# Two-layer attention kernel: for some query tiles the maxima of the first two key chunks are taken as a + relu(b − a) in one pass of VectorE

## The chip, the core and the metric

One NeuronCore of a Trainium2 chip runs the whole program. The time is device microseconds (us) from start to end of one execution; a figure for a kernel is the median of several. The profile is of one execution and has its own time. Engines: PE is TensorE, which multiplies matrices into PSUM banks of 128 x 512 fp32; DVE is VectorE, ACT is ScalarE, POOL is GpSimd, SP only issues DMAs.

## The reference

Four blocks in a row on x of 2048 tokens by 512: A, B, A, B with the same weights. B (a router that sends two tokens through a small feed-forward net) matters here only because two rows of x, and with them two keys, are known late.

```python
# A: attention of 32 heads of 16, one shared key and value head (x is already normalised)
q = (x @ wq).reshape(B, S, H, Dh).transpose(0, 2, 1, 3)
k = x @ wk
v = x @ wv
scores = einsum("bhqd,bkd->bhqk", q, k) * (Dh ** -0.5)
p = softmax(scores, axis=-1)
o = einsum("bhqk,bkd->bhqd", p, v)
return o.transpose(0, 2, 1, 3).reshape(B, S, H * Dh) @ wo
```

## The kernel before

`layer` runs one A and one B block; it is called twice. A layer has 32 units `u` (4 query chunks x 4 groups of heads x 2) of 16 steps each, so 512 steps `t` of about 2.5 us.

The softmax subtracts each row's exact maximum, so every score is computed twice:

- **Maxima.** `max_mm(mi, n)` multiplies 128 queries by one chunk of 512 keys (`CW`) into a bank of the pool `psM` (4 banks), and VectorE reads the bank and reduces it to one column of the tile `mx` (L404, L406). There are four key chunks; a tile `mi` holds two of them for two halves of the rows: even `mi` have chunks 0 and 1, odd `mi` chunks 2 and 3. `n` from 0 to 3 gives the half and the chunk: the half is `h = 1 - n % 2`, the chunk `2 * (mi % 2) + n // 2`. Half 0 lies on the array's rows 0 to 47, half 1 on rows 64 to 111.
- **`max_parts`** (L414) takes the largest of the four chunks on VectorE and splits it in two parts on GpSimd (L419, L420); **`max_rows`** turns it on TensorE (L426), copies it on ScalarE (L428) and sends it by SP's DMA into two more rows of `q_st` (L432), so that the next product subtracts the maximum by itself.
- **Scores.** `scores(t, i)` computes keys by queries into a bank of `psS` (3 banks, L453), and ScalarE takes the exponential into `pr` (L455). Quarter `i` of a step lies on half `i % 2` of the rows.
- **`pv_mm`** multiplies by the values into `pO` (L482). **`between`** puts pieces of other projections (queries of the next unit, output projection; L187) on TensorE.

The order is written by hand. A step has four quarters `i`; each issues one `scores` and then one max product of the tile that is `LEAD` = 12 steps ahead (`made(mi) = mi - 12` from tile 16 on). After every third quarter (`RUN` = 3, counted over the whole layer as `4 * t + i`) come `pv_mm` for three halves of `pr` and perhaps one piece. So TensorE's work goes in *runs*: three pairs (score product, max product), then `pv_mm`, then perhaps a piece. The two products of a pair lie on different halves of the rows.

Before step 0 of a layer, eight steps issue max products alone; `first` gives the order of the first ones. Between the layers `layer` waits for B's two tokens and then corrects two columns of the keys (L1177 to L1188) and of the values (L1196, L1197).

Keys: `kv_piece` computes a chunk into `kvs[c]`, `k_store` writes it to DRAM, `k_spread` reads it back in six DMAs of SP into the rows of `k_sts`.

Of the kernel before, what the change touches and what calls it, by code (L numbers as in the profile page):

```python
# [9 lines left out]
F32 = mybir.dt.float32  # L10
BF = mybir.dt.bfloat16
FR = mybir.dt.float32r
U32 = mybir.dt.uint32
AF = mybir.ActivationFunctionType
OP = mybir.AluOpType
# [30 lines left out]
HALVES = 3  # L46

# [7 lines left out]
def interleaved_layers(ctx, tc, x_in, wq, wkv, wo, w_r, w_gate, w_up, w_down, out):  # L55
# [57 lines left out]
    k_sts = [work.tile([P, S], FR, name="k_st", bufs=2) for _ in range(2)]  # L113

    x2_d = dram.tile([S, D], F32, name="x2_d")
    z_d = [dram.tile([2 * TPC, CW], F32, name=f"z_d{i}") for i in range(2)]
    zr_d = [dram.tile([2 * TPC, CW], F32, name=f"zr_d{i}") for i in range(2)]
    k_d = [dram.tile([P, 2, P], F32, name=f"k_d{i}") for i in range(NCH)]
# [169 lines left out]
    def k_spread(li, c):  # L288

        for i in range(2 * NSLOT):  # L290
            n, h = divmod(i, 2)
            r = h * HR + n * DH
            src = k_d[c].rearrange("(j x) m t -> x m j t", j=TPC)[:DH, n // 2]
            dst = k_sts[li][r:r + DH, c * CW:(c + 1) * CW].bitcast(F32).rearrange("x (j t) -> x j t", j=TPC)
            nc.sync.dma_start(dst, src)

    def kv_v(li, c):
        kf = kvs.pop(c)[0]
        pv = aux([P, TPC, 2 * DH], F32)
        nc.tensor.transpose(pv.rearrange("p j x -> p (j x)"), kf, ident)  # L300
        nc.scalar.copy(v_exts[li][:, c * TPC:(c + 1) * TPC, 1:32:2], pv[:, :, DH:])
# [60 lines left out]
    def layer(li, src_d, dst_d, early=None):  # L362
# [26 lines left out]
        mx, mi = {}, 0  # L389

        def max_mm(mi, n):
            u, i = divmod(mi, 16)
            if i == 0 and n == 0:
                mx[u] = work.tile([P, 4, 16], F32, name="mx", bufs=3)
            pm = bank()
            nq = cuts[u]

            b, r = divmod(i, 16 // nq)
            x, c = divmod(r, 2)
            j, s = divmod(x, 4 // nq)  # L400
            h, c = 1 - n % 2, 2 * c + n // 2
            q = (b * 4 // nq + s) * P
            r = slice(h * HR, h * HR + KQ)
            nc.tensor.matmul(pm, q_st[u][r, j, q:q + P], k_st[r, c * CW:(c + 1) * CW], start=True, stop=True)  # L404
            i = b * 16 // nq + h * 8 // nq + 2 * s + j
            nc.vector.reduce_max(mx[u][:, c, i:i + 1], pm, axis=AX.X)  # L406
# [388 lines left out]
        for c in range(NCH):  # L795
# [31 lines left out]
            for b in range(TPC):  # L827
# [9 lines left out]
                if li == 0:  # L837
                    t += 4 if c < NCH - 2 else 3
                    at(t, next_x, i, nc.gpsimd)
                    at(t + 2, ln_t, i)  # L840
                    if b == TPC - 1:
                        at(t + 4, whole, kv_piece, c)
                        at(t + 6, k_store, li + 1, c)
                        at(t + 6, kv_v, li + 1, c)
                        at(t + 8, k_spread, li + 1, c)
        wd, wu = [], []

        def load_wd(n):
# [5 lines left out]
            else:  # L854
                for k in range(2):
                    if n == 3:
                        w = work.tile([P, D], F32, name="so0", bufs=8)
                    elif n < 6:
                        w = work.tile([P, D], F32, name=("qh", "ql")[n - 4])
                    else:  # L860
                        w = work.tile([P, D], F32, name="wd", bufs=4)
# [64 lines left out]
        first[12:12] = [(4, n) for n in range(4)]  # L926
# [3 lines left out]
        for t in range(-LEAD0, last):  # L930
# [4 lines left out]
            mms = [(m, n) for m in tiles for n in range(4)]  # L935
            mms = [first[4 * m + n] if 4 * m + n < len(first) else (m, n) for m, n in mms]
# [230 lines left out]
        for tok in toks:  # L1167
            of = nc.snap(tok // P)
            xb.append((of, work.tile([P, NDC, P], F32, name="xh", bufs=3)))
            nc.gpsimd.tensor_copy(xb[-1][1], xT[:, :, bass.ds(of * P, P)])  # L1170
        q_st.clear()
# [20 lines left out]
        q_stack(0, 0, w, engs=both)  # L1192
        for of, x in xb:
# [42 lines left out]
    in_stats(g4, g4)  # L1236
    kv_v(0, 1)
# [7 lines left out]
    def early():  # L1245
# [3 lines left out]
        kv_v(0, 3)  # L1249
        k_spread(0, 3)  # L1250

# [32 lines left out]
```

## Time and profile before

| | |
|---|---|
| time, median of 3 runs | 2792.49 us (2791.6 to 2792.81) |
| the profiled execution: its own time, and its span | 2793.8 us, 2792.0 us |
| busy share of PE, PE's weight loads, DVE, ACT, POOL | 99%, 57%, 93%, 82%, 26% |
| mean granted TensorE clock | 0.985 |
| max products and their reductions | 4096 of each |

The span runs from the first to the last instruction; 1.8 us of the execution lie outside it. The ends of matrix products are modelled, so PE's 99% doesn't say that it runs at its peak. The stream of steps takes about 60 to 1340 us in the first layer and 1450 to 2730 us in the second; between them and at the end stand the B blocks.

### The profile page before, as it was taken

The numbers are of one execution on the slowest core, as the hardware profiler recorded it, in microseconds if no ns is written. First come the engines' busy times: TensorE is split into PE (matmuls) and PEld (weight loads), VectorE is DVE, ScalarE is ACT, GpSimd is POOL, SyncE is SP. The second block draws the span as 40 slices with busy tenths as digits, with TensorE's granted clock in tenths as the row PEclk, the third lists the DMA queues.
The fourth block names the chain that finished last, engine by engine and source line by source line (L and its number), as shares of the span: only waits on it lengthen the run. The fifth ranks groups of instructions, "written<-read, shape, count | busy, mean of one in ns | idle before, by whom it ended". The sixth has DMA issues, their size and how long they took to land. (4 is left out here: it accounts for less than half of the span.)

```text
span 2792.0 us, 94326 instructions
## 1 busy us (share of the span) xinstructions
PE 2755.8 (99%) x39761; PEld 1602.5 (57%) x39761; DVE 2607.0 (93%) x4496; ACT 2294.5 (82%) x4705; POOL 720.3 (26%) x1756
## 2 busy tenths in 40 slices
PE   7999999999999999999999999999999999999999
PEld 4655555555555555555656555555555555555555
DVE  7999999999999999999669999999999999999994
ACT  2888888888888888888718888888888888888884
POOL 2100002022451116525510000021124421154262
PEclk8999999999999999999969999999999999999999
DMA  3011110000110001111400000100001100110113
GB/s 110 8 31 34 40 56 18 19 13 19 43 44 18 16 18 48 37 35 42 132 25 9 20 20 20 30 19 16 18 14 51 35 15 20 31 41 22 35 54 122
DMA packets 71386, 97.68 MB, mean 35 GB/s; under 512 B 22732, under 2 KB 32396, under 8 KB 70964
## 3 DMA queue, kind: packets, MB, share of 16 engines
q1 hardware_dynamic: 68098, 89.84, 11.2%
q8 instruction: 313, 5.13, 0.8%
q10 hardware_dynamic: 2354, 1.61, 0.2%
q14 instruction: 109, 0.89, 0.1%
q0 software_dynamic: 512, 0.20, 0.0%
HBM read 43.68 MB, written 17.77 MB: 22 GB/s over the span
## 5 line engine op out<-in xcount | busy, mean ns | idle before, releaser
L406 DVE TENSOR_REDUCE mx<-pM 128x1 f32<-128x512 f32 x4096 | 2508.5, 682 | 84.9 <-PE pM L404 67.5
L455 ACT ACTIVATE pr<-pS 128x512 f32<-128x512 f32 x4044 | 2133.6, 603 | 322.1 <-PE pM L404 232.9
L404 PE MATMUL pM<-k_st,q_st 48*128 48x512 f32 x4096 | 1390.5, 443 | 5.4 <-DVE mx L406 2.4
L453 PE MATMUL pS<-q_st,k_st 50*128 50x512 f32 (+1 forms) x4248 | 1357.2, 422 | 4.6 <-DMA q_st<-mr 2.2
L482 PE MATMUL pO<-pr,v_ext 128*32 128x128 f32 (+1 forms) x22528 | 1175.4, 328 | 2.2 <-ACT so L488 1.9
L453 PEld LDWEIGHTS pS<-q_st,k_st 50*128 50x128 f32 x4248 | 683.1, 186 | 468.4 <-ACT pr L455 265.9
L482 PEld LDWEIGHTS pO<-pr,v_ext 128*32 128x32 f32 x22528 | 562.6, 109 | 527.0 <-issue 347.8
L404 PEld LDWEIGHTS pM<-k_st,q_st 48*128 48x128 f32 x4096 | 669.0, 187 | 33.6 <-DVE mx L406 27.5
L419 POOL CAST mp<-ma 128x8 fp32r<-128x8 f32 (+1 forms) x136 | 26.0, 191 | 834.7 <-PE pM L404 460.9
L613 POOL TENSOR_TENSOR x<-x,qf 128x128 f32<-128x128 f32 x128 | 58.6, 459 | 545.0 <-ACT qf L612 545.0
L187 PE MATMUL pO<-xT,wq_sb 128*32 128x128 f32 x3584 | 180.0, 273 | 0.0
L345 POOL CAST qh<-qf 128x128 fp32r<-128x128 f32 x120 | 34.8, 290 | 513.4 <-ACT qf L344 483.3
L187 PE MATMUL pO<-wo_sb,so 128*32 128x128 f32 x2816 | 137.1, 273 | 0.0
L187 PEld LDWEIGHTS pO<-xT,wq_sb 128*32 128x32 f32 x3584 | 111.3, 110 | 34.0
L634 POOL TENSOR_TENSOR xh<-xh 128x128 f32<-128x128 f32 (+7 forms) x384 | 98.1, 255 | 30.1
L187 PEld LDWEIGHTS pO<-wo_sb,so 128*32 128x32 f32 x2816 | 86.7, 110 | 24.1
L696 POOL TENSOR_TENSOR xh<-xh 128x256 f32<-128x256 f32 (+8 forms) x216 | 66.6, 308 | 15.0
L428 ACT COPY mr<-pM 16x128 f32<-16x128 f32 (+1 forms) x136 | 34.6, 255 | 31.0 <-DVE mx L406 18.0
L346 POOL TENSOR_TENSOR ql<-qf,qh 128x128 fp32r<-128x128 f32 x120 | 55.0, 459 | 9.7
L488 ACT COPY so<-pO 128x256 f32<-128x256 f32 (+1 forms) x136 | 52.6, 387 | 2.1 <-PE pO L482 2.1
L680 POOL TENSOR_SCALAR xh<-x,mv,rs 128x512 f32<-128x512 f32 x24 | 49.9, 2077 | 0.0
L187 PE MATMUL pS<-wo_sb,so 128*32 128x128 f32 (+1 forms) x896 | 44.2, 330 | 0.0
(251 smaller groups left out, 940.5 us busy)
## 6 DMA issues: line engine op xcount, KB each, us to landing
q_st<-qh SPq DMA_DIRECT2D x244, 64.0 KB
q_st<-mr SPq DMA_DIRECT2D x512, 2.0 KB
q_st<-ql SPq DMA_DIRECT2D x122, 64.0 KB
zt<-zr_d SPq DMA_DIRECT2D x120, 64.0 KB
xl_d<-xh SPq DMA_DIRECT2D x28, 256.0 KB
pr<-in_w_up SPq DMA_DIRECT2D x12, 448.0 KB
x<-in_x SPq DMA_DIRECT2D x20, 256.0 KB
x_d<-x SPq DMA_DIRECT2D x16, 256.0 KB
```

Of the source, the lines that this page charges most:

```text
L187: nc.tensor.matmul(out[r], lhsT[:, r], rhs, start=start, stop=stop, skip_group_check=shared)
L346: nc.gpsimd.tensor_tensor(ql, qf, qh.bitcast(F32), op=OP.subtract)
L404: nc.tensor.matmul(pm, q_st[u][r, j, q:q + P], k_st[r, c * CW:(c + 1) * CW], start=True, stop=True)
L406: nc.vector.reduce_max(mx[u][:, c, i:i + 1], pm, axis=AX.X)
L453: nc.tensor.matmul(ps[:, k * 2 * w:(k + 1) * 2 * w], k_st[rows, kt * P:(kt + 1) * P], q_st[u][rows, :, b * w:(b + 1) * w], start=True, sto ...
L455: nc.scalar.activation(pr[hs][:, h, :], ps, AF.Exp)
L482: nc.tensor.matmul(po[u][32 * j:32 * (j + 1), b * w + q.start:b * w + q.stop], v_ext[:, kt, 1 - u % 2:33 - u % 2], p[:, j % 2, k, j // 2, ...
L488: nc.scalar.copy(so[u][:, b * w:(b + 1) * w], po[u][:, b * w:(b + 1) * w])
L613: nc.gpsimd.tensor_tensor(x1[i][:, w], x1[i][:, w], y, op=OP.add)
L634: g.tensor_tensor(t[:, :n], t[:, :n], t[:, n:2 * n], op=OP.add)
L680: eng.tensor_scalar(xl, x1[i], mv2[m][:, b, 0:1], rs2[m][:, b:b + 1], op0=OP.subtract, op1=OP.mult)
L696: nc.gpsimd.tensor_tensor(rp_t[i][:, :n], rp_t[i][:, :n], rp_t[i][:, n:2 * n], op=OP.add)
```

## The change

In some tiles the maximum of chunks 0 and 1 of a half is no longer found by two reductions. A fifth key chunk `k_dif` holds key chunk 1 minus key chunk 0. The product with it gives b − a; ScalarE writes relu(b − a) to the tile `over` in SBUF; the ordinary product with chunk 0 gives a; one `tensor_tensor_reduce` on VectorE adds `over` to it and reduces the sum by max: a + relu(b − a) is max(a, b). GpSimd sets the unused column of `mx` to -3e38. `pairs(mi)` says for how many halves of a tile this is done: one (half 1) for every sixth tile from 20 to 494, in both layers, and both halves for the eight even tiles below 16 in the second layer. In such tiles the order of `n` becomes 2, 0, 1, 3 or 2, 0, 3, 1. `first` of the second layer is rearranged so that tiles 0 and 2 come last. `k_dif` is made on GpSimd, stored and spread by SP like a chunk of keys, and its two late columns are corrected between the layers by products of their own (`xd`, `pd`, `kdn`). Three weight tiles of `load_wd` move to other buffers.

```diff
 RUN = 3
 HALVES = 3
 
+PAIR = 6
+PAIRED = 0, 16
...
     k_sts = [work.tile([P, S], FR, name="k_st", bufs=2) for _ in range(2)]
+    k_difs = [work.tile([P, CW], FR, name="k_dif", bufs=2) for _ in range(2)]
...
-    def k_spread(li, c):
+    def spread(of, dst):
 
         for i in range(2 * NSLOT):
             n, h = divmod(i, 2)
-            src = k_d[c].rearrange("(j x) m t -> x m j t", j=TPC)[:DH, n // 2]
-            nc.sync.dma_start(dst, src)
+            src = of.rearrange("(j x) m t -> x m j t", j=TPC)[:DH, n // 2]
+            nc.sync.dma_start(dst[r:r + DH].bitcast(F32).rearrange("x (j t) -> x j t", j=TPC), src)
+    def k_spread(li, c):
+        spread(k_d[c], k_sts[li][:, c * CW:(c + 1) * CW])
+
+    dif = []
+
+    def k_dif():
+
+        d = work.tile([P, P], F32, name="qf")
+        nc.gpsimd.tensor_tensor(d, kvs[1][0], dif.pop(), op=OP.subtract)
+        dif.append(d)
+
+    def k_dif_parts():
+        kf = dif.pop()
+        dif.append(work.tile([P, 2, P], FR, name="kp", bufs=1))
+        nc.gpsimd.tensor_copy(dif[0][:, 0, :], kf)
+        nc.gpsimd.tensor_tensor(dif[0][:, 1, :], kf, dif[0][:, 0, :].bitcast(F32), op=OP.subtract)
+
+    def k_dif_store():
+        nc.sync.dma_start(kd_d, dif.pop().bitcast(F32))
+
+    def k_dif_spread(li):
+        spread(kd_d, k_difs[li])
 
     def kv_v(li, c):
         kf = kvs.pop(c)[0]
+        if c == 0:
+            dif.append(kf)
         pv = aux([P, TPC, 2 * DH], F32)
...
+        mx, mi, over = {}, 0, {}
+
+        def pairs(mi):
+
+            c = mi % 2
+            if c:
+                return 0
+            if mi < PAIRED[li]:
+                return 2
+            return int(mi >= 16 and mi % PAIR == 2 and mi < 16 * (NU - 1))
+
+        def column(u, i, n):
+
             nq = cuts[u]
             b, r = divmod(i, 16 // nq)
             x, c = divmod(r, 2)
             j, s = divmod(x, 4 // nq)
             h, c = 1 - n % 2, 2 * c + n // 2
-            q = (b * 4 // nq + s) * P
+            return h, c, j, (b * 4 // nq + s) * P, b * 16 // nq + h * 8 // nq + 2 * s + j
+
+        def max_mm(mi, n):
+            u, i = divmod(mi, 16)
+            if u not in mx:
+                mx[u] = work.tile([P, 4, 16], F32, name="mx", bufs=3)
+                for m in range(16):
+                    for half in range(pairs(16 * u + m)):
+                        j = column(u, m, half)[-1]
+                        nc.gpsimd.memset(mx[u][:, 1, j:j + 1], -3.0e38)
+            pm = bank()
+            h, c, j, q, i = column(u, i, n)
+            two = c < 2 and h >= 2 - pairs(mi)
             r = slice(h * HR, h * HR + KQ)
-            nc.tensor.matmul(pm, q_st[u][r, j, q:q + P], k_st[r, c * CW:(c + 1) * CW], start=True, stop=True)
-            i = b * 16 // nq + h * 8 // nq + 2 * s + j
-            nc.vector.reduce_max(mx[u][:, c, i:i + 1], pm, axis=AX.X)
+            k = k_difs[li][r] if two and c else k_st[r, c * CW:(c + 1) * CW]
+            nc.tensor.matmul(pm, q_st[u][r, j, q:q + P], k, start=True, stop=True)
+            if two and c:
+                over[mi, h] = work.tile([P, CW], F32, name="over", bufs=2)
+                nc.scalar.activation(over[mi, h], pm, AF.Relu)
+            elif two:
+                o = over.pop((mi, h))
+                nc.vector.tensor_tensor_reduce(o, pm, o, 1.0, -3.0e38, OP.add, OP.max, mx[u][:, 0, i:i + 1])
+            else:
+                nc.vector.reduce_max(mx[u][:, c, i:i + 1], pm, axis=AX.X)
 
...
                         at(t + 6, k_store, li + 1, c)
                         at(t + 6, kv_v, li + 1, c)
                         at(t + 8, k_spread, li + 1, c)
+                        if c == 1:
+                            at(t + 5, k_dif)
+                            at(t + 8, k_dif_parts)
+                            at(t + 9, k_dif_store)
+                            at(t + 11, k_dif_spread, li + 1)
...
-                    if n == 3:
+                    if n == 3 or n == 7 and k == 0:
                         w = work.tile([P, D], F32, name="so0", bufs=8)
                     elif n < 6:
                         w = work.tile([P, D], F32, name=("qh", "ql")[n - 4])
+                    elif n == 6:
+                        w = work.tile([P, D], F32, name="over", bufs=2)
                     else:
-                        w = work.tile([P, D], F32, name="wd", bufs=4)
+                        w = work.tile([P, D], F32, name="k_dif", bufs=2)
...
         first = [(2 * j + c // 2, c % 2 * 2 + h) for c in range(NCH) for j in range(2) for h in range(2)]
-        first[12:12] = [(4, n) for n in range(4)]
+        late = [(2 * j, n) for j in range(2) for n in (2, 0, 3, 1)]
+        first = [f for f in first if f not in late] + [(4, 2), (4, 0), (4, 3), (4, 1)] + late
...
-            mms = [(m, n) for m in tiles for n in range(4)]
-            mms = [first[4 * m + n] if 4 * m + n < len(first) else (m, n) for m, n in mms]
+            mms = [(m, n) for m in tiles for n in ((0, 1, 2, 3), (2, 0, 1, 3), (2, 0, 3, 1))[pairs(m)]]
+            done = 4 * mi - len(mms)
+            mms = [first[done + k] if done + k < len(first) else f for k, f in enumerate(mms)]
             for i in range(4):
                 if t >= 0:
                     scores(t, i)
...
+        xd = work.tile([P, NDC, 2], F32, name="xd", bufs=1)
+        cols = [nc.snap(tok % CW) for tok in toks]
+        for k, col in enumerate(cols):
+            nc.gpsimd.tensor_tensor(xd[:, :, k:k + 1], xT[:, :, bass.ds(col + CW, 1)], xT[:, :, bass.ds(col, 1)], op=OP.subtract)
...
         q_stack(0, 0, w, engs=both)
+        pd = aux([P, 2], F32)
+        for k in range(NDC):
+            nc.tensor.matmul(pd, wkv_sb[:, k, :], xd[:, k, :], start=k == 0, stop=k == NDC - 1)
+        kdf, kdn = work.tile([P, 2], F32, name="kdf", bufs=1), work.tile([P, 2], FR, name="kdn", bufs=1)
+        nc.scalar.copy(kdf, pd)
+        nc.gpsimd.tensor_copy(kdn, kdf)
+        k_lo(kdn, kdf, nc.gpsimd)
+        for k, col in enumerate(cols):
+            nc.gpsimd.tensor_copy(k_difs[li + 1][:, bass.ds(col, 1)], kdn[:, k:k + 1])
...
+    k_dif()
     kv_v(0, 1)
     k_spread(0, 1)
...
         kv_v(0, 3)
+        k_dif_parts()
         k_spread(0, 3)
+        k_dif_store()
+        k_dif_spread(0)
```

## Rows read from the trace of the kernel before

**Rows 1.** The page's first part: busy time, share of the span and number of instructions of each engine.

```profile
PE 2755.8 (99%) x39761; PEld 1602.5 (57%) x39761; DVE 2607.0 (93%) x4496; ACT 2294.5 (82%) x4705; POOL 720.3 (26%) x1756
```

**Rows 2.** The page's costliest groups: line, engine, operation, out<-in, count | busy us, mean ns of one | idle time before them and what ended most of it.

```profile
L406 DVE TENSOR_REDUCE mx<-pM 128x1 f32<-128x512 f32 x4096 | 2508.5, 682 | 84.9 <-PE pM L404 67.5
L455 ACT ACTIVATE pr<-pS 128x512 f32<-128x512 f32 x4044 | 2133.6, 603 | 322.1 <-PE pM L404 232.9
L404 PE MATMUL pM<-k_st,q_st 48*128 48x512 f32 x4096 | 1390.5, 443 | 5.4 <-DVE mx L406 2.4
```

**Rows 3.** VectorE's line of time, a stretch in the first query chunk and two in a later one: start us, length us, what, how many merged, and in brackets the idle time before it and what ended it.

```profile
200.12 18.30 DVE L406 TENSOR_REDUCE mx<-pM 128x1 f32<-128x512 f32 x30
...
509.46 7.49 DVE L406 TENSOR_REDUCE mx<-pM 128x1 f32<-128x512 f32 x12 [0.24 <-PE pM L404]
...
543.60 5.48 DVE L406 TENSOR_REDUCE mx<-pM 128x1 f32<-128x512 f32 x9 [0.24 <-PE pM L404]
```

**Rows 4.** The reductions of L406 alone, by stretches of 100 us: stretch, its length, VectorE's busy time in them (how many), granted clock, DMA share, GB/s.

```profile
200.00:300.00 100.00, 98.94 (x165) 1.00 0.12 32
...
500.00:600.00 100.00, 96.94 (x158) 1.00 0.08 19
```

**Rows 5.** The waits of TensorE's weight loads from 75 to 1340 us (the first layer's stream): who waited for whom, us in total, times, longest.

```profile
PEld pS L453 <- ACT pr L455: 131.3, 509, 0.7
...
PEld pM L404 <- DVE mx L406: 1.7, 8, 0.4
```

**Rows 6.** The same from 1464 to 2730 us (the second layer's stream).

```profile
PEld pS L453 <- ACT pr L455: 134.3, 520, 0.7
...
PEld pM L404 <- DVE mx L406: 2.2, 10, 0.4
```

**Rows 7.** TensorE's line of time over three runs in a later chunk: L453 are score products, L404 max products, L482 the products with the values, L187 a piece of a projection.

```profile
525.83 0.50 PE L453 MATMUL pS<-q_st,k_st 50*128 50x512 f32 x1
...
527.41 0.40 PE L187 MATMUL pO<-wo_sb,so 128*32 128x128 f32 x8
527.75 0.50 PE L453 MATMUL pS<-q_st,k_st 50*128 50x512 f32 x1
527.75 0.49 PE L404 MATMUL pM<-k_st,q_st 48*128 48x512 f32 x1
528.08 0.40 PE L453 MATMUL pS<-q_st,k_st 50*128 50x512 f32 x1
528.09 0.39 PE L404 MATMUL pM<-k_st,q_st 48*128 48x512 f32 x1
528.32 0.40 PE L453 MATMUL pS<-q_st,k_st 50*128 50x512 f32 x1
528.32 0.40 PE L404 MATMUL pM<-k_st,q_st 48*128 48x512 f32 x1
528.65 0.64 PE L482 MATMUL pO<-pr,v_ext 128*32 128x256 f32 x8
...
529.44 0.50 PE L453 MATMUL pS<-q_st,k_st 50*128 50x512 f32 x1
...
531.13 0.50 PE L453 MATMUL pS<-q_st,k_st 50*128 50x512 f32 x1
```

**Rows 8.** Products and weight loads (PEld) of the first two pairs of a run.

```profile
241.37 0.18 PEld L453 LDWEIGHTS pS<-q_st,k_st 50*128 50x128 f32 x1 [0.20 <-issue]
241.37 0.50 PE L453 MATMUL pS<-q_st,k_st 50*128 50x512 f32 x1
...
241.38 0.73 PE L404 MATMUL pM<-k_st,q_st 48*128 48x512 f32 x2
241.48 0.42 PEld L453 LDWEIGHTS pS<-q_st,k_st 50*128 50x128 f32 x2
```

**Rows 9.** VectorE's line of time in the B block: an instruction that reads a PSUM bank and an SBUF tile of 512 and accumulates, and what follows it.

```profile
1389.29 0.69 DVE L998 SCALAR_TENSOR_TENSOR x<-pS,x 128x512 f32<-128x512 f32 x1 [2.67 <-PE pS L187]
...
1390.03 0.15 DVE L999 TENSOR_SCALAR top<-top 128x1 f32<-128x1 f32 x1
```

**Rows 10.** ScalarE's line of time: exponentials back to back.

```profile
243.79 3.26 ACT L455 ACTIVATE pr<-pS 128x512 f32<-128x512 f32 x6 [0.17 <-PE pM L404]
```

**Rows 11.** ScalarE's one load of a table of functions in the whole execution (group).

```profile
L258 ACT ACT_TABLE_LOAD x1 | 1.3, 1283 | 1.8 <-issue 1.8
```

**Rows 12.** VectorE's line of time at the start of the second layer.

```profile
1430.05 9.65 DVE L406 TENSOR_REDUCE mx<-pM 128x1 f32<-128x512 f32 x16
...
1439.83 9.68 DVE L406 TENSOR_REDUCE mx<-pM 128x1 f32<-128x512 f32 x16
...
1449.51 7.26 DVE L406 TENSOR_REDUCE mx<-pM 128x1 f32<-128x512 f32 x12
```

**Rows 13.** TensorE's line of time between the layers: the correction of the keys, and the first max products after it.

```profile
1417.34 1.87 PE L1177 MATMUL pM<-xn,wkv_sb 128*128 128x2 f32 x8
...
1424.52 0.79 PE L404 MATMUL pM<-k_st,q_st 48*128 48x512 f32 x2
```

**Rows 14.** SP's line of time at the start of the first layer: the spreading of the keys, and the next DMA after it.

```profile
26.90 13.57 SPq L295 DMA_DIRECT2D k_st<-k_d  x21
47.85 0.57 SPq L359 DMA_DIRECT2D q_st<-qh  x1
```

**Rows 15.** A small memset on GpSimd (group).

```profile
L97 POOL MEMSET code<- 128x3 f32 x1 | 0.1, 100 | 0.0
```

More of the change, by code (lines that the diff above doesn't have):

```diff
@@ L117, in interleaved_layers @@
     zr_d = [dram.tile([2 * TPC, CW], F32, name=f"zr_d{i}") for i in range(2)]
+    kd_d = dram.tile([P, 2, P], F32, name="kd_d")
     k_d = [dram.tile([P, 2, P], F32, name=f"k_d{i}") for i in range(NCH)]
@@ L292, in k_spread @@
             r = h * HR + n * DH
-            src = k_d[c].rearrange("(j x) m t -> x m j t", j=TPC)[:DH, n // 2]
-            dst = k_sts[li][r:r + DH, c * CW:(c + 1) * CW].bitcast(F32).rearrange("x (j t) -> x j t", j=TPC)
-            nc.sync.dma_start(dst, src)
+            src = of.rearrange("(j x) m t -> x m j t", j=TPC)[:DH, n // 2]
[16 more added lines that the diff above has]
+        spread(kd_d, k_difs[li])
     def kv_v(li, c):
         kf = kvs.pop(c)[0]
+        if c == 0:
+            dif.append(kf)
         pv = aux([P, TPC, 2 * DH], F32)
@@ L386, in layer @@
         cuts = [cut(u) for u in range(NU)]
[L389 to L395, printed above, removed]
+        mx, mi, over = {}, 0, {}
[7 more added lines that the diff above has]
+        def column(u, i, n):
             nq = cuts[u]
```

## Prediction

> **What bounds the kernel now.** I read the shares and the groups of the page first, then stretches of VectorE's and TensorE's lines of time, then the waits of TensorE's weight loads.
>
> The shares leave two candidates: PE is 99% busy and DVE 93% [rows 1], and most of DVE is the 4096 reductions that the change is about [rows 2]. VectorE is nearly full. In the first query chunk it takes 30 reductions in 18.30 us without a gap, 0.61 us each; in a later chunk it stops for 0.24 us after every nine to twelve, and each time it waits for TensorE's product [rows 3]. Per 100 us it does 165 reductions early (0.606 us each, its own pace) and 158 later [rows 4].
>
> TensorE is full as well, and it waits for VectorE hardly at all. Over the first layer's stream its weight loads waited 8 times, 1.7 us in all, for a bank that a reduction had to free, over the second 10 times, 2.2 us [rows 5, 6]. What they do wait for, often and shortly, is ScalarE's exponential, 509 and 520 times [rows 5, 6]. Most of that is hidden, because a weight load runs ahead of its product: TensorE's line of time shows its runs laid end to end. A run with a piece begins at 525.83 and the next at 527.75, 1.92 us; one without begins at 529.44 and the next at 531.13, 1.69 us [rows 7]. Three reductions take 1.83 us, between the two. So TensorE gains on VectorE in runs without a piece and loses in runs with one, and with four banks between them the two come out nearly even: early they are level, later TensorE sets the pace. A relief of VectorE alone is therefore worth little, and anything added to TensorE costs about its full length.
>
> **The change, part by part.** From 20 to 494 every sixth tile is 80 tiles, one pair each, in two layers: 160 pairs. Eight even tiles with two pairs add 16. Of 4096 reductions 352 go; 176 relus on ScalarE and 176 add-and-max on VectorE come; the number of products stays 4096.
>
> *VectorE.* Two reductions are 1.21 us at the pace of [rows 3]. No row shows the new instruction. The nearest reads a bank and an SBUF tile of 512 and accumulates: it starts at 1389.29 and the next real instruction at 1390.03, so 0.74 us [rows 9]. It can hardly take less than one reduction, 0.61, and at 1.21 it would save nothing. I take 0.74: 0.47 us saved per pair (0.60 to 0), 176 pairs, 83 us of VectorE. What TensorE gets of it is only its waits for VectorE, 3.9 us in the two streams [rows 5, 6]: −4 us, from 0 to −8, should the view name only half of them.
>
> *TensorE's order.* This is the term that decides. The two products of a pair start together, 527.75 and 527.75, 528.08 and 528.09, 528.32 and 528.32, because they lie on different halves of the rows; the pairs follow each other by 0.33 and 0.24 us, and the value product by another 0.33 [rows 7]. The score products of a step lie on halves 0, 1, 0, 1. The max products lay on 1, 0, 1, 0; in the order n = 2, 0, 1, 3 they lie on 1, 1, 0, 0. Which quarters share a run? A pair tile 6k + 2 is worked at step t = 6k − 10, and 4t leaves the same remainder by three as t, which is 2: its quarter 0 is the last of one run, quarters 1 to 3 are the next. Quarter 0 has halves 0 and 1 as before. The next run has 1, 1; 0, 0; 1, 0. Half 1's second product must wait for the first; half 0's first starts beside it; then half 0's second beside half 1's third; then half 0's third alone. That is four places in time instead of three. A place costs 0.24 us by the inner distance, 0.33 by the outer, 0 if something hides it. I take 0.24, since the added place has others before and behind it: 160 × 0.24 = +38 us (0 to +53). In the 16 pairs at the second layer's start TensorE has time to spare.
>
> Here the Trainium skill would charge more: "TensorE: Matmul & The Clock Gate", The mechanism, has weight loads overlap running products only where the row group differs. By that rule each of the two new same-half neighbours would also expose a load, and at the load's 0.18 us [rows 8] the sum would be 160 × 0.36 = 58 us higher. The rows speak against it: loads for the second pair start at 241.48, while the first pair's products, on the same halves, run from 241.37 for 0.50 us [rows 8].
>
> *What swallows part of it.* The extra place falls into runs some of which already wait, mostly for ScalarE; there it replaces a wait. Against 131 and 134 us of such waits of loads [rows 5, 6] I let a fifth of the 38 vanish: −8 (0 to −20).
>
> *ScalarE.* An exponential of the same size comes every 0.53 us back to back (six in 3.26 us) [rows 10], and I price the relu like it. It stands between the exponentials of quarters 0 and 1. Three exponentials are 1.6 us in a run of 1.69 to 1.92; with a relu 2.1 in a run that has grown to 1.93 to 2.16. So the exponentials come about 0.2 us late only where the run has no piece, and three score banks absorb some. One pair in six at 0.2 is +5 us (0 to +32, each pair at 0.2). No row shows a relu. A load of function tables before and after each would add 176 × 2.6 = 458 us; the trace has one load in all, though exponentials, copies and squares take turns [rows 11], so I price none. The Trainium skill, "ScalarE: Activation LUTs", Table sets, has relu in every set, which no run here shows yet.
>
> VectorE's add-and-max stands in line behind the relu, and the reductions of the same tile behind it. The relu ends some 0.7 us after the exponentials of its run, about when the product with chunk 0 is ready; what waits on VectorE is covered by the 0.47 us that it saves, and the bank comes free before TensorE is round the four. I add nothing.
>
> *Start of the second layer.* There VectorE does set the pace: 16, 16 and 12 reductions in three stretches with only a small instruction between [rows 12], 44 of them, 11 tiles, six even, 12 pairs: 12 × 0.47 = −6 us (0 to −9 for 16 pairs and a cheaper instruction). Ahead of the first max product, TensorE gets a product `pd` of the form of L1177, which took 1.87 us, in line between it and the 1424.52 of the first max product [rows 13]: +2. The other small steps on GpSimd (`xd`, `kdn`) run beside it.
>
> *The rest.* In the first layer SP has issued the keys by 40.5 us and isn't needed before 47.85 [rows 14]; a store and six more DMAs at 0.65 us (21 in 13.57) are 4.5 us and a round trip. That just fits: +0.5 (0 to 2). In mid-layer the same seven stand ahead of the rows of maxima on SP once; the maxima are sent steps ahead of their use, so nothing (0 to 3). The memsets at 0.1 us [rows 15] run on GpSimd, 26% busy [rows 1], a whole block of tiles before `max_parts` asks for them.
>
> Sum: 38 − 4 − 8 + 5 − 6 + 2 + 0.5 = +27.5 on the profiled execution's 2793.8, 2821.3; the median of the runs is 1.3 lower, so **2820 us**, 1.0% slower.
>
> **The rivals.**
>
> *VectorE sets the pace after all* (faster). For it speaks its full line in the first query chunk [rows 3, 4]: 128 tiles, so 21 pairs a layer, 42 in both. If the added place is hidden, these give 42 × 0.47 = 20 us, and with the −4, −6 and +7.5 of the other terms the time is 2793.8 − 1.3 − 22.5 = 2770. It decides where the place costs less than the 0.47 that VectorE saves and finds a wait to fill. Against it: the 3.9 us of waits. The Trainium skill would go further. "Perfetto Trace Analysis", Identifying the Most-Contended Engine, names the engine of highest occupancy and judges TensorE by its weight loads, here 57%; that makes it VectorE at 93%, and 176 × 0.47 would give about 2710. The gaps in [rows 3], ended by TensorE, are against that rule in this kernel. Chance 0.16.
>
> *The place costs nothing and VectorE's time is worth nothing*: −4 + 5 − 6 + 2.5 is −2.5, 2790 us, no change. It speaks for it that the outer distance of a run, 0.33, holds 0.09 of slack and that a wait can swallow the rest. Chance 0.14.
>
> *ScalarE becomes the bound*: each pair loses 0.2 to the relu besides its place, nothing is swallowed: 38 + 32 − 4 − 6 + 2.5 = +62, 2855 us. For it, the thousand short waits; against it, ScalarE's 82%. Chance 0.08.
>
> The forecast has 0.62. That the change doesn't do what it says I leave out: the code removes the 352 reductions.
>
> **How the numbers follow.** The likeliest case alone runs from 2806 (half the place swallowed) to 2836 (0.33 a place). The range is 2778 to 2842: it leaves out most of the ScalarE case and the better half of the VectorE case, with some tails 0.18. Faster or slower by under 0.2%, 5.6 us, is about what a measurement of this kernel can't tell from no change. Slower 0.62 + 0.08 = 0.70, same 0.14, faster 0.16.
>
> **What would show it.** Right: runs of about 1.93 or 2.15 us where a pair tile's quarters 1 to 3 stand, with two products of one half 0.24 us apart; reductions per 100 us, a pair counted as two, down from 158 to about 156; VectorE's share down to near 90% with longer gaps ended by TensorE; ScalarE's up by some 3 points. Wrong: runs with a pair no longer than others, then one of the first two rivals; waits of score loads for ScalarE far above 131 us, then the third; an add-and-max much over 0.74 us would move the VectorE terms.

## The result: 0.9% slower, with another mechanism than the one forecast

The changed kernel takes 2817.61 us (median, 2816.6 to 2818.58) against 2792.13 us for the kernel before on the same chip: ratio 1.0091, 95% interval 1.0074 to 1.0109, +25.5 us. The profiled execution took 2816.6 us, its span 2814.8 us, at the same granted clock of 0.985. The forecast was 2820. The sum came out; its largest term did not show when it was tested by itself, and a term put at 5 us was worth 21 to 25. So the number is right by luck. The rest of this text is about that.

The page's shares and groups of the kernel after (columns as in [rows 1, 2]; L459 is the reduction, L457 the add-and-max, L454 the relu, L451 the max product, L506 the score product, L508 the exponential, L535 the value product, L192 the pieces):

```profile
PE 2776.9 (99%) x39769; PEld 1613.2 (57%) x39769; DVE 2512.9 (89%) x4496; ACT 2356.3 (84%) x4882; POOL 729.5 (26%) x1945
...
L508 ACT ACTIVATE pr<-pS 128x512 f32<-128x512 f32 x4044 | 2136.1, 609 | 288.3 <-PE pM L451 216.5
L459 DVE TENSOR_REDUCE mx<-pM 128x1 f32<-128x512 f32 x3744 | 2298.3, 682 | 58.6 <-PE pM L451 42.8
...
L457 DVE CUSTOM_DVE_ANT_0 over<-pM,over 128x512 f32<-128x512 f32 x176 | 121.7, 692 | 136.7 <-PE pM L451 73.0
...
L454 ACT ACTIVATE over<-pM 128x512 f32<-128x512 f32 x176 | 111.3, 633 | 11.6 <-PE pM L451 7.1
```

352 reductions have gone and VectorE is down from 93% to 89%. ScalarE is up by 62 us; its 176 relus are 111.3 us when counted by themselves, and overlap the instructions beside them. No further table load shows on ScalarE (one in the whole execution, as in [rows 11]), so the relu needed none; that agrees with what the Trainium skill, "ScalarE: Activation LUTs", Table sets, says of it.

The weight loads' waits for a score bank in the whole execution after (us in total, times, longest); before, the same line is 265.9 us, 1031 times:

```profile
PEld pS L506 <- ACT pr L508: 284.8, 1106, 0.5
```

**Where it is lost.** ScalarE's busy time in four stretches, the first query chunk of each layer (100 to 370, 1490 to 1770) and the later ones. Columns: stretch, its length, ScalarE's busy time (instructions), granted clock, DMA share, GB/s. First the kernel before:

```profile
100.00:370.00 270.00, 238.93 (x485) 1.00 0.12 33
400.00:1330.00 930.00, 803.40 (x1646) 1.00 0.10 29
1490.00:1770.00 280.00, 247.59 (x502) 1.00 0.07 17
1800.00:2720.00 920.00, 796.42 (x1630) 1.00 0.10 28
```

and after:

```profile
100.00:370.00 270.00, 239.88 (x493) 1.00 0.12 31
400.00:1330.00 930.00, 819.35 (x1695) 1.00 0.10 29
1490.00:1770.00 280.00, 248.19 (x512) 1.00 0.07 17
1800.00:2720.00 920.00, 811.76 (x1678) 1.00 0.10 27
```

In the first chunk ScalarE was 88.5% busy before (238.93 of 270) and is 88.8% after, although every sixth tile now brings a relu: the relus displaced exponentials instead of filling gaps. Later it was at 86.4% and rose to 88.1%: there most of the relus found a gap. The page's 82% [rows 1] hid this, because it counts the B blocks.

The exponentials themselves say the same: both traces have all 4096 of them, and the lateness of each against its counterpart in the kernel before, worked out from their starts, grows by 4.5 and 6.9 us over the first chunks of the two layers, by 5.2 and 4.9 us over their three later chunks each, and by 0.7 us between the layers; with 0.5 us at the first one that is 22.7 of the 22.8 us between the two spans (2814.8 and 2792.0). In the first layer, lateness grows by 0.27 us around a relu of the first chunk (median of 20) and by 0.05 us around a later one (median of 60). The exponentials are late, not slower: where one follows another without a gap, it starts 0.49 us behind it in both kernels (mean).

### The profile page after: what moved, and what is told of

Its sections match the earlier page's. It is cut to its first block, busy times and chain, and to the rows that moved or that the text cites. A ratio compares the mean times of both kernels' runs of the same rounds, so it can differ in the third digit from the quotient of the medians.

```text
span 2814.8 us, 94920 instructions
## 1 busy us (share of the span) xinstructions
PE 2776.9 (99%) x39769; PEld 1613.2 (57%) x39769; DVE 2512.9 (89%) x4496; ACT 2356.3 (84%) x4882; POOL 729.5 (26%) x1945
## 5 line engine op out<-in xcount | busy, mean ns | idle before, releaser
L508 ACT ACTIVATE pr<-pS 128x512 f32<-128x512 f32 x4044 | 2136.1, 609 | 288.3 <-PE pM L451 216.5
L459 DVE TENSOR_REDUCE mx<-pM 128x1 f32<-128x512 f32 x3744 | 2298.3, 682 | 58.6 <-PE pM L451 42.8
L506 PE MATMUL pS<-q_st,k_st 50*128 50x512 f32 (+1 forms) x4248 | 1360.5, 428 | 4.3 <-DMA q_st<-mr 0.5
L451 PE MATMUL pM<-k_st,q_st 48*128 48x512 f32 x3920 | 1299.7, 440 | 3.2 <-DVE mx L459 1.3
L535 PE MATMUL pO<-pr,v_ext 128*32 128x128 f32 (+1 forms) x22528 | 1175.3, 328 | 2.1 <-ACT so L541 1.9
L506 PEld LDWEIGHTS pS<-q_st,k_st 50*128 50x128 f32 x4248 | 668.2, 186 | 485.0 <-ACT pr L508 284.8
L535 PEld LDWEIGHTS pO<-pr,v_ext 128*32 128x32 f32 x22528 | 562.5, 109 | 516.6 <-issue 337.8
L451 PEld LDWEIGHTS pM<-k_st,q_st 48*128 48x128 f32 x3920 | 623.5, 187 | 30.3 <-DVE mx L459 18.3
L457 DVE CUSTOM_DVE_ANT_0 over<-pM,over 128x512 f32<-128x512 f32 x176 | 121.7, 692 | 136.7 <-PE pM L451 73.0
L192 PE MATMUL pO<-xT,wq_sb 128*32 128x128 f32 x3584 | 180.0, 273 | 0.0
L192 PE MATMUL pO<-wo_sb,so 128*32 128x128 f32 x2816 | 137.0, 273 | 0.0
L192 PEld LDWEIGHTS pO<-xT,wq_sb 128*32 128x32 f32 x3584 | 111.3, 110 | 34.0
L454 ACT ACTIVATE over<-pM 128x512 f32<-128x512 f32 x176 | 111.3, 633 | 11.6 <-PE pM L451 7.1
L192 PEld LDWEIGHTS pO<-wo_sb,so 128*32 128x32 f32 x2816 | 86.6, 110 | 24.1
L451 PE MATMUL pM<-k_dif,q_st 48*128 48x512 f32 x176 | 78.3, 449 | 2.5 <-ACT over L454 1.3
```

Source lines behind the costliest of these rows:

```text
L192: nc.tensor.matmul(out[r], lhsT[:, r], rhs, start=start, stop=stop, skip_group_check=shared)
L451: nc.tensor.matmul(pm, q_st[u][r, j, q:q + P], k, start=True, stop=True)
L454: nc.scalar.activation(over[mi, h], pm, AF.Relu)
L457: nc.vector.tensor_tensor_reduce(o, pm, o, 1.0, -3.0e38, OP.add, OP.max, mx[u][:, 0, i:i + 1])
L506: nc.tensor.matmul(ps[:, k * 2 * w:(k + 1) * 2 * w], k_st[rows, kt * P:(kt + 1) * P], q_st[u][rows, :, b * w:(b + 1) * w], start=True, sto ...
L508: nc.scalar.activation(pr[hs][:, h, :], ps, AF.Exp)
```

## The experiments

Four theories. **A**: the added place in TensorE's order, the forecast's +38. **B**: VectorE, standing behind the relu, holds up the reductions. **C**: ScalarE's time, each relu makes the exponentials behind it late. **D**: the bank of differences is held until the relu has read it. The kernel before ran at 2793.1 to 2793.4 us beside them; each ratio below is against it, with its 95% interval.

**The order alone.** The kernel before, with the new order of the max products in every sixth tile and nothing else.

```diff
-            if i == 0 and n == 0:
+            if u not in mx:
...
-            mms = [(m, n) for m in tiles for n in range(4)]
+            mms = [(m, n) for m in tiles for n in ((2, 0, 1, 3) if m % 6 == 2 and 16 <= m < 16 * (NU - 1) else range(4))]
```

> The kernel before with one thing of the change: the max products of every sixth tile are issued in the order 2, 0, 1, 3, with four ordinary reductions and no difference chunk. Theory A (the prediction: two products of one half in a row cost TensorE a place of 0.24 us): 160 times 0.24, about +38 us, 2830. Theory B (the order costs nothing; what costs is VectorE standing at the add-and-max until the relu has come): within 4 us of the kernel before, 2792.

2794.94 us, 1.0006 (0.9997 to 1.0016). The order costs 1.5 us, 4.5 at the upper bound, where A has 38. Why, the trace of the change itself shows: TensorE's line of time at such a run, whose products the program has in the order score (half 1), max (half 1), score (half 0), max (half 0), score (half 1), max (half 0):

```profile
270.12 0.50 PE L506 MATMUL pS<-q_st,k_st 50*128 50x512 f32 x2
270.46 0.40 PE L451 MATMUL pM<-k_st,q_st 48*128 48x512 f32 x2
270.69 0.40 PE L506 MATMUL pS<-q_st,k_st 50*128 50x512 f32 x1
270.70 0.39 PE L451 MATMUL pM<-k_st,q_st 48*128 48x512 f32 x1
271.02 0.86 PE L535 MATMUL pO<-pr,v_ext 128*32 128x128 f32 x16
```

Two score products begin together at 270.12, then two max products at 270.46, then the last two at 270.69: while the first max product waited for its half, the second score product, which comes after it in the program, began on the other half. Three places, 0.90 us from 270.12 to the value product, as in [rows 7] (527.75 to 528.65). That the program has the other order, the semaphore that TensorE's finished products count up bears out in the trace: one count comes at 270.63, three at 270.87 to 270.94, two at 271.11 and 271.14. By these the second score product is reported only after the first max product, although it began 0.34 us earlier. The Trainium skill, "TensorE: Matmul & The Clock Gate", The mechanism, has matmuls start and end strictly in program order; by these starts that doesn't hold for the start of products on different halves, while the reports of their ends here do come in that order.

**The add-and-max one or two products later.** B would shrink with both. With the order 2, 1, 0, 3 the halves alternate as before, so the place of A would go too; with 2, 1, 3, 0 it would stay.

```diff
-            mms = [(m, n) for m in tiles for n in ((0, 1, 2, 3), (2, 0, 1, 3), (2, 0, 3, 1))[pairs(m)]]
+            mms = [(m, n) for m in tiles for n in ((0, 1, 2, 3), (2, 1, 0, 3), (2, 0, 3, 1))[pairs(m)]]
```

> The change with the order 2, 1, 0, 3 in the tiles with one pair: the halves alternate as before, and one ordinary reduction stands between the relu and the add-and-max. Theory A: the place of 38 us goes and a swallowed wait comes back, about 2787. Theory B: the wait of 0.8 us ahead of each add-and-max falls to about 0.2, the loss in the first query chunk goes, 2793 give or take 6.

With 2, 1, 3, 0 in that place:

> The change with the order 2, 1, 3, 0: two ordinary reductions stand between the relu and the add-and-max, but the halves are 1, 0, 0, 1, and a run again has products of one half in a row. Theory A: four places instead of three, so no better than the change, 2818. Theory B: the wait is gone, 2788 give or take 6, not slower than the order 2, 1, 0, 3.

2815.26 us, 1.0080 (1.0063 to 1.0097), and 2823.99 us, 1.0113 (1.0097 to 1.0130). One later, VectorE's wait for the relu is all but gone. The group of the add-and-max in that kernel:

```profile
L457 DVE CUSTOM_DVE_ANT_0 over<-pM,over 128x512 f32<-128x512 f32 x176 | 119.9, 682 | 10.7 <-ACT over L454 9.7
```

Its idle time fell from 136.7 to 10.7 us and the time by 2 to 3 us, less than the intervals tell apart. Waits of VectorE that vanish without the time moving were not on the path: B falls. A falls once more as well, since without the place it has 2787. Two later is slower still. Its trace shows where: in the later chunks of the first layer, the run with quarters 1 to 3 of a pair tile takes 2.11 us (mean, start to start of the runs) where it takes 1.99 with one later. In the run that starts at 541.34, the third score product is the second one on its half, but its load starts only at 541.80, when an exponential has ended (541.75), and the run has four places. Whether that holds for all of them, no run here settles.

**No add-and-max.** The add-and-max becomes an ordinary reduction of chunk 0, so that nobody waits for the relu (the maximum of chunk 1 is left out).

```diff
-                o = over.pop((mi, h))
-                nc.vector.tensor_tensor_reduce(o, pm, o, 1.0, -3.0e38, OP.add, OP.max, mx[u][:, 0, i:i + 1])
+                over.pop((mi, h))
+                nc.vector.reduce_max(mx[u][:, 0, i:i + 1], pm, axis=AX.X)
```

> The change in its own order 2, 0, 1, 3, with the relu, but the add-and-max is an ordinary reduction of chunk 0: this leaves chunk 1 out of the maximum of those pairs. VectorE no longer waits for ScalarE; TensorE's order and ScalarE's work are those of the change. Theory A: TensorE's places remain, 2815. Theory B: 2786 give or take 6. A third theory, that the relu on ScalarE delays the exponentials: remains near 2815 with more waits of score loads for ScalarE than in the kernel before.

2815.09 us, 1.0080 (1.0063 to 1.0097): nobody waits for the relu, and the loss is still there. That is against B once more.

**No relu.** The product of differences is made and read by nobody; the add-and-max adds a tile of weights that is always there (so chunk 1 is left out of the maximum).

```diff
-                over[mi, h] = work.tile([P, CW], F32, name="over", bufs=2)
-                nc.scalar.activation(over[mi, h], pm, AF.Relu)
+                pass
             elif two:
-                o = over.pop((mi, h))
-                nc.vector.tensor_tensor_reduce(o, pm, o, 1.0, -3.0e38, OP.add, OP.max, mx[u][:, 0, i:i + 1])
+                o = work.tile([P, CW], F32, name="over", bufs=2)
+                nc.vector.tensor_tensor_reduce(o, pm, wq_sb[:, 0, :], 1.0, -3.0e38, OP.add, OP.max, mx[u][:, 0, i:i + 1])
```

> The change without its relus: the product with the difference chunk is read by nobody, and the add-and-max adds a constant tile of SBUF, so chunk 1 is left out of the maximum of those pairs. VectorE does the work of the change and never waits for ScalarE. Theory C: 2790 give or take 5. If the loss came from the difference product, its bank, the add-and-max or the steps between the layers, it stays near 2815.

2792.86 us, 0.9998 (0.9989 to 1.0008). The whole loss goes with the relu: 24.8 us between this kernel and the change. And it shows the other half of the balance: 352 reductions fewer, with everything else of the change in place, gain nothing that can be told from noise (0.1%).

**The relu without the relief.** The product goes with chunk 1 itself, all 4096 reductions stay, and the 176 relus write a tile nobody reads.

```diff
...
-            k = k_difs[li][r] if two and c else k_st[r, c * CW:(c + 1) * CW]
+            k = k_st[r, c * CW:(c + 1) * CW]
...
-            elif two:
-                o = over.pop((mi, h))
-                nc.vector.tensor_tensor_reduce(o, pm, o, 1.0, -3.0e38, OP.add, OP.max, mx[u][:, 0, i:i + 1])
-            else:
-                nc.vector.reduce_max(mx[u][:, c, i:i + 1], pm, axis=AX.X)
+            nc.vector.reduce_max(mx[u][:, c, i:i + 1], pm, axis=AX.X)
```

> The change with its relus and its order, but chunk 1 itself in place of the difference chunk and all 4096 ordinary reductions, so that VectorE does what it did before; the relus' results are used by nobody. Theory C (the relu pushes ScalarE's exponentials back, and TensorE's score products wait for their banks): about +24 us over the kernel before, 2817, most of it in the first query chunk of each layer. Theory A and B (TensorE's order, VectorE's wait): 2796, the small steps between the layers alone.

2870.42 us, 1.0278 (1.0260 to 1.0295), three times the loss of the change. It is no clean measure of the relu: relu and reduction read the same bank, and the trace puts the reduction behind the relu. VectorE's waits from 75 to 1340 us in it:

```profile
DVE mx L451 <- ACT over L450: 56.8, 79, 1.1
```

So C, which had 2817 here, is not tested by it; a VectorE without relief has no room for such waits.

**A fourth score bank, taken from the maxima** (`psM` 3, `psS` 4), before and after the change. If the loss is a late exponential, a fourth score bank should absorb it.

```diff
-    psM = ctx.enter_context(tc.tile_pool(name="psM", bufs=4, space=bass.MemoryType.PSUM))
-    psS = ctx.enter_context(tc.tile_pool(name="psS", bufs=3, space=bass.MemoryType.PSUM))
+    psM = ctx.enter_context(tc.tile_pool(name="psM", bufs=3, space=bass.MemoryType.PSUM))
+    psS = ctx.enter_context(tc.tile_pool(name="psS", bufs=4, space=bass.MemoryType.PSUM))
```

> The kernel before with four banks for scores and three for maxima in place of three and four. Theory C says that score products wait for the exponential of the third product before: with a fourth bank these waits shrink, but VectorE has one bank less to work ahead on. 2760 to 2810; TensorE's waits for ScalarE below 131 us a layer, those for VectorE above 2 us.

> The change with four banks for scores and three for maxima. Theory C: the relus' delay is taken up by the fourth bank, so the change costs less than 8 us against the kernel before with the same banks, and may be faster. If the relu costs in another way, the difference stays 24 us.

2933.01 us, 1.0500 (1.0482 to 1.0517), and 2976.55 us, 1.0658 (1.0640 to 1.0676). Both far from what was expected, and inconclusive for C: taking one of the maxima's four banks costs 140 us, although the scores got one more. The loads' waits of the first, 75 to 1340 us, beside [rows 5]:

```profile
PEld pS L453 <- ACT pr L455: 52.2, 183, 0.4
PEld pM L404 <- DVE mx L406: 47.3, 194, 0.5
```

The score waits do fall from 131.3 to 52.2 us, but 1.7 us of waits for reductions become 47.3. The change on top costs 43.5 us here, with the bank of differences now waited for as well (12.6 us in the same stretch).

**A relu that only takes ScalarE's time.** As without the relu, but ScalarE computes the relu of a tile of weights in SBUF that nobody waits for. C keeps its cost, D has none (chunk 1 is again left out).

```diff
-                over[mi, h] = work.tile([P, CW], F32, name="over", bufs=2)
-                nc.scalar.activation(over[mi, h], pm, AF.Relu)
+                r_ = work.tile([P, CW], F32, name="over", bufs=2)
+                nc.scalar.activation(r_, wq_sb[:, 0, :], AF.Relu)
...
```

> As the change without relus (the difference product read by nobody, the add-and-max over a constant tile, so chunk 1 left out of those maxima), but ScalarE does a relu of 128 x 512 from SBUF to SBUF at the same place of its line, which nobody waits for. It takes ScalarE's time and holds no bank. Theory C (ScalarE's time pushes the exponentials back): 2810 give or take 5. Theory D (what costs is the bank of the difference product, held until the relu has read it): 2793, like the change without relus.

2813.82 us, 1.0069 (1.0053 to 1.0086). 20.7 of the loss of 24.8 us come back with ScalarE's time alone (14.8 to 24.0 by the interval): C. This relu even takes 0.52 us of ScalarE from its start to that of an exponential right behind it, where the one of the change takes 0.48 (medians). D, which had none, falls as the main cause. Some 4 us remain for D, for B and for the start of the second layer together; the interval hardly tells them from nothing.

**Half a relu.** ScalarE reads 256 of the 512 columns; the add-and-max adds the tile of weights (chunk 1 left out).

```diff
-                nc.scalar.activation(over[mi, h], pm, AF.Relu)
+                nc.scalar.activation(over[mi, h][:, :CW // 2], pm[:, :CW // 2], AF.Relu)
...
```

> The change with relus of 256 columns in place of 512, and a constant tile added in place of the relu's result (chunk 1 left out of those maxima); VectorE still waits for the relu. The relu takes about 0.25 us of ScalarE in place of 0.48. Theory C: half the loss or less, 2796 to 2806. Theory D: the bank is held almost as long, 2813.

2799.48 us, 1.0020 (1.0010 to 1.0029): +6.4 us, a quarter of the loss. From a relu's start to that of an exponential right behind it are 0.29 us here and 0.48 in the change (medians), so the cost isn't in proportion to ScalarE's time. That a short relu fits into gaps that a long one overruns would explain this; it is a reading, not a test.

**Pairs only in the later chunks**, from tile 144.

```diff
-            return int(mi >= 16 and mi % PAIR == 2 and mi < 16 * (NU - 1))
+            return int(mi >= 144 and mi % PAIR == 2 and mi < 16 * (NU - 1))
```

> The change with single pairs only from tile 144 on, so none in the first query chunk, where runs without a piece follow each other and ScalarE's exponentials are closest to the limit (58 of 80 pairs a layer stay). Theory C: a pair costs about 0.1 us there and 0.33 in the first chunk, so 2 x 58 x 0.1 = 12 of the 25 us stay: 2805. If every pair cost the same, 2811.

2804.88 us, 1.0038 (1.0026 to 1.0051). Leaving out 42 of the 160 single pairs (59 a layer stay, not the expected 58) takes away 12.7 us against the change, or 13.7 if each is taken against the kernel before that ran beside it: 0.30 to 0.33 us for each. The other 118 and the 16 at the start cost the remaining 11.8 us, 0.1 each. That is the split that the lateness of the exponentials and ScalarE's busy share by stretches show.

**Rows of maxima one step earlier**, in the kernel before, for a version that would be faster.

```diff
-                at(e + 2, max_rows, u, b)
+                at(e + 1, max_rows, u, b)
```

> The kernel before with the rows of maxima turned and sent one step earlier. The score products that wait for these rows, once a unit by about 0.25 us, should stop waiting: 64 x 0.25 = 16 us at most, 2780 to 2792; slower than 2796 if TensorE then waits for VectorE and GpSimd at the turning instead.

2793.37 us, 0.9999 (0.9989 to 1.0008). The score products' waits for these rows went (1.0 us in the first layer's stream), and the loads' waits for reductions grew from 1.7 to 5.9 us there. No kernel here beats the one before.

## Why the prediction came out

**What a relu does**, in three steps of the trace after. ScalarE's line of time at a pair of the first chunk:

```profile
251.92 1.57 ACT L508 ACTIVATE pr<-pS 128x512 f32<-128x512 f32 x3 [0.40 <-PE pM L451]
253.37 0.30 ACT L373 ACTIVATE qf<-pO 128x128 f32<-128x128 f32 x1
253.53 0.41 ACT L541 COPY so<-pO 128x256 f32<-128x256 f32 x1
253.78 1.64 ACT L508 ACTIVATE pr<-pS 128x512 f32<-128x512 f32 x3
255.22 0.69 ACT L454 ACTIVATE over<-pM 128x512 f32<-128x512 f32 x1
255.70 3.15 ACT L508 ACTIVATE pr<-pS 128x512 f32<-128x512 f32 x6
259.62 4.95 ACT L508 ACTIVATE pr<-pS 128x512 f32<-128x512 f32 x9 [0.77 <-PE pM L451]
```

Two short instructions (0.41 us from 253.37 to 253.78) and the relu (0.48 us from 255.22 to 255.70) follow each other within 2 us, and from 251.92 to 258.85 ScalarE has no gap. TensorE's weight loads of the same stretch:

```profile
254.99 0.19 PEld L506 LDWEIGHTS pS<-q_st,k_st 50*128 50x128 f32 x2 [0.41 <-ACT pr L508]
...
255.47 0.18 PEld L506 LDWEIGHTS pS<-q_st,k_st 50*128 50x128 f32 x1 [0.18 <-ACT pr L508]
...
257.43 0.18 PEld L506 LDWEIGHTS pS<-q_st,k_st 50*128 50x128 f32 x1 [0.31 <-ACT pr L508]
```

The third load waits 0.31 us for an exponential, in the run behind the pair, and its products start late. TensorE in that run, from its first score product (256.69) to its value product (257.86) and the first score product behind the next piece:

```profile
256.69 0.50 PE L506 MATMUL pS<-q_st,k_st 50*128 50x512 f32 x1
...
257.86 1.08 PE L535 MATMUL pO<-pr,v_ext 128*32 128x128 f32 x24
...
259.08 0.50 PE L506 MATMUL pS<-q_st,k_st 50*128 50x512 f32 x1
```

The same work without the relu: ScalarE's stretch from 249.74, the third load's wait (0.17 us), and TensorE in the same run.

```profile
249.74 1.57 ACT L507 ACTIVATE pr<-pS 128x512 f32<-128x512 f32 x3 [0.40 <-PE pM L451]
...
251.60 5.01 ACT L507 ACTIVATE pr<-pS 128x512 f32<-128x512 f32 x9
257.16 4.96 ACT L507 ACTIVATE pr<-pS 128x512 f32<-128x512 f32 x9 [0.55 <-PE pM L451]
...
254.97 0.18 PEld L505 LDWEIGHTS pS<-q_st,k_st 50*128 50x128 f32 x1 [0.17 <-ACT pr L507]
...
254.50 0.50 PE L505 MATMUL pS<-q_st,k_st 50*128 50x512 f32 x1
...
255.41 1.07 PE L534 MATMUL pO<-pr,v_ext 128*32 128x128 f32 x24
...
256.63 0.50 PE L505 MATMUL pS<-q_st,k_st 50*128 50x512 f32 x1
```

The run takes 1.17 us to its value product with the relu and 0.91 without. From 249.74 to the score product at 256.63 are 6.89 us; after, from 251.92 to the same product at 259.08, 7.16. So 0.27 us of the relu's 0.48 are lost here, and ScalarE's gap behind it grows from 0.55 to 0.77 us: the time that TensorE has lost, it can't win back, and the gap that follows is of no use.

Step by step:

- **What bounds the kernel**: half right. That relief of VectorE is worth little held (without the relu: 0.9998). Wrong was the picture of ScalarE. The forecast read VectorE by stretches and ScalarE only by its share of the whole; in the first chunk it is nearly as full as in any run here (88.5%; 89.4% with the add-and-max two later, 241.42 of 270, is the most). That "three score banks absorb some", and that one pair in six is late, was taken from no row.
- **VectorE's 0.74 us**: a reduction follows the add-and-max after 0.62 us, the cheap end of the range. It was of no consequence, as the forecast said of VectorE's time. VectorE at that run:

```profile
271.00 0.69 DVE L457 CUSTOM_DVE_ANT_0 over<-pM,over 128x512 f32<-128x512 f32 x1 [0.83 <-PE pM L451]
271.62 0.08 DVE L457 DVE_READ_ACCUMULATOR2_ANT mx<- 128x1 f32 x1
271.62 2.48 DVE L459 TENSOR_REDUCE mx<-pM 128x1 f32<-128x512 f32 x4
```

- **TensorE's order, +38**: this step failed, measured at +1.5 (−0.8 to +4.5). The assumption was that a product which waits for its half holds up the next one on the other half. The forecast's own sign of it, a run with a pair no longer than others, showed it: 0.90 us, and over the first layer's trace of the order alone the runs that begin with two score products take 0.91 us to their value product, like the others (medians). The −8 swallowed fell with it. With the order 2, 1, 3, 0 a run does show four (541.34).
- **ScalarE, +5 (0 to +32)**: mis-sized; 21 to 25, 20.7 of it by ScalarE's time alone. A relu's length (0.48 us where 0.53 was taken, from a stretch that has the last exponential's whole length in it) was about right; "only where the run has no piece" and "some absorbed" were wrong in the first chunk, where a pair pays some 0.3 us on the mean, and nearer the mark later, at 0.1. It is the third rival's mechanism, which had a chance of 0.08, with 21 to 25 of the 32 us that it gave the relu and without the place.
- **The signs to look for** did not tell the two apart. VectorE's share fell to 89% and ScalarE's rose by 2 points, as forecast, with another cause. The reductions per 100 us, a pair counted as two, did not fall in a later stretch (500 to 600: 146 and 6 add-and-max, so 158 as before), but in the first chunk (200 to 300: 161 where there were 165). The sign of the third rival was badly chosen: score loads' waits "far above 131 us". They rose to 140.4 us in the first layer's stream and by 18.9 us in all, and not where the time went: in the first chunk of the first layer they are 37.7 us before (75 to 375) and 38.9 after (75 to 380). A load runs ahead of its product, so its wait is no measure of TensorE's lost time. ScalarE's busy share by stretches is.
- **VectorE behind the relu, 0**: right (the two runs against B).
- **Start of the second layer, −6**: VectorE waits there for a relu that stands behind ScalarE's own DMA issues, so the gain went: from the layer's first reduction to its first score product are 24.8 us before, 21.3 without the relu, 24.1 after. ScalarE, then VectorE:

```profile
1444.98 0.60 ACTq L388 DMA_DIRECT2D q_st<-qh  x1
1445.63 1.08 ACT L454 ACTIVATE over<-pM 128x512 f32<-128x512 f32 x2 [4.17 <-DMA q_st<-qh]
...
1446.26 0.69 DVE L457 CUSTOM_DVE_ANT_0 over<-pM,over 128x512 f32<-128x512 f32 x1 [1.95 <-ACT over L454]
```

- **`pd`, +2**: it is in line, as forecast; without the relu the layer's first reduction starts 2.7 us later than before (1428.05 where it was 1425.35), 0.6 of it carried over from the first layer:

```profile
1430.99 1.87 PE L1261 MATMUL pS<-xd,wkv_sb 128*128 128x2 f32 x8
```

- **The range**: by the forecast's own sum half the place swallowed gives 2809 and not 2806, and 0.33 a place 2835 and not 2836; nothing hangs on either.

Without the relu, +1.5 for the order, about +2 for `pd` and −3.5 at the second layer's start make nothing, and −0.3 was measured. The relu takes the rest, 24.8 us, found as a difference; 20.7 of it were measured by ScalarE's time alone. That 38 − 8 + 5 and 1.5 + 24.8 differ little is chance.

The Trainium skill, "ScalarE: Activation LUTs", Rules for kernel authors, advises VectorE rather than ScalarE for a relu. That points the way the runs point, for a reason of this kernel: VectorE's time was free (0.9998 for 352 reductions fewer) and ScalarE's was not. No run here has the relu on VectorE, where a pair would again take two instructions of VectorE.

## What to carry to other kernels

An engine's share of the whole execution says little about the stage where work is added to it: read the busy share of *every* engine that gets work by stages, also of one that looks like it has room. A sum that comes out right proves none of its terms; test the largest by itself, as one edit of the order alone did here. And relief of an engine that nobody waits for is worth nothing, while work on one in a closed loop with the bounding engine costs what the loop has no gap for: here over half of a relu's 0.48 us in the first chunk, and a fifth of it later.

## What the runs showed of the hardware that was not expected

- Two matrix products on different halves of the rows start out of program order when the earlier one has to wait for its half (270.12 before 270.46), and are reported as finished in program order; reordering them by hand cost 1.0006.
- The fused add-and-max on VectorE, with its accumulator, runs at close to a plain reduction's pace, 0.62 us for 512 columns where a reduction takes 0.61; the reading of its accumulator (0.08 us) starts together with the next reduction, at 271.62, and adds nothing to that.
- Banks between TensorE and VectorE are worth more here than the waits suggest: with three instead of four the kernel takes 140 us (5.0%) more, although the scores got one more, while the loads' waits for reductions grew by 100.4 us (27.5 to 127.9 in the whole execution) and their waits for exponentials fell by 156.5 (265.9 to 109.4).
